# The low part of a weight one step after its cast, and the drain of attention in hand order

## The chip, the cores and the metric

The kernel runs on one core of one Trainium2 chip. The metric is the device time of one execution in microseconds (us). Before the change its median over three runs is 1068.23 us.

## The reference, cut to what matters

Attention with a position bias feeds two feed-forward layers:

```python
scores = q @ k.T * scale + bias(pos)                  # 4 batches, 8 heads, 576 x 576, head size 64
x = softmax(scores) @ v                               # 2304 tokens x 512
h = x @ w_in                                          # 512 -> 2048
g = (a0 + a1*h + a2*h**2 + a3*h**3) / (1 + |b0|*|h| + |b1|*h**2 + 1e-6)
y = g @ w_out                                         # 2048 -> 512
z = maximum(maximum(y @ w1, y @ w2), y @ w3) @ w_out2 # 512 -> 768 -> 512
```

The weights come in double precision, and the matrix products are wanted in full single precision.

## The kernel before

**Precision.** A weight or an activation is split in a high part (a cast to the matmul's format) and a low part (value minus high part). Each product is three matmuls: high times high, high times low, low times high.

**Attention** is a sequence of 80 units, one per batch, pair of heads p and tile of 128 rows t (the last tile, t = 4, holds 64 rows of two heads). `attn_tick(n)` issues the work of tick n in the order of the list `KN['A2']`: scores of unit n (`sc`), a part of an attention-times-value product (`av`), the transposes of unit n-2 (`T`), bias and minimum of unit n (`r0`, `r1`, VectorE), the reciprocal of unit n-1's sums and its spreading on GpSimd (`n`), the exponentials (`e0`, `e1`, ScalarE), and the copies of the transposes out of PSUM (`v0`, `v1`). At the end of a tick come the weights' step, and in ticks 72, 75 and 80 the load and the two splits of the first block's x (`split_x`, L446: a cast on ScalarE, a subtraction on GpSimd for each of four chunks).

**First layer.** `ffn_tick(n)` is one step for chunk f of a block of tokens: the 12 matmuls `ph` of chunk n (`ffn_h`), the 12 matmuls `y` of chunk n-2 (`ffn_y`), then the rational function: `rat_poly(n)`, the cast and low part of g of the chunk before (`rat_split(n-1)`), `rat_inv(n)` and `rat_newton(n)`, and at the end the weights' step. So on ScalarE a step is three activations of `rat_poly`, the cast to gs (L506), Ln, Exp and the weights' instructions; on GpSimd it is the low part of gs (L507) and then the weights' low parts.

**Drain.** After tick 79 no new unit starts, but five more ticks finish the last units. They are ticks 80 to 84, and in each of them `attn_tick(n)` is followed by `ffn_tick(n - 80)`. Both run a weights' step, so there are two weights' steps in such a tick; here they are called a (at the end of the attention's part) and f (at the end of the layer's part).

**Weights.** `weights_tick(new)` advances every weight that is under way by one stage and then starts `new` further loads. Its four stages are: load into one of three raw buffers (SyncE's DMA queue); for a weight in double precision an activation on ScalarE and a shift on VectorE (`rebias`, L387, L388), which need the landed load; joining the two words on VectorE (`join`, L396); then the cast on ScalarE and the low part on GpSimd or VectorE (`parts`, L402). The weights w_in (`wi`, 16 of them) are loaded narrowed already, so their second and third stages are empty; w_out (`wo`, 16) has all four. A raw buffer comes free when the low part is made. The loads of `wi` start in tick 64, one a tick; `wo` follows them. `weights_flush` runs further weights' steps if a chunk's weight isn't there.

**Order.** SyncE's queue is always in program order (L76). Inside `ordered(3)` PE, VectorE, GpSimd and ScalarE are too. Ticks 0 to 79 and the layer's steps from 5 on stand in it; the drain does not, and there a planner that works with modelled times chooses the order on these four engines. Each engine's own queue is then worked off in that order.

**Places.** `big` has two buffers, which hold the transposed attention tiles `at` and, later, the working pair g of the rational function; `slot` has 35 buffers of 4,608 bytes a partition for weights, keys, bias, exponentials and x; `bank` has four PSUM banks for scores' transposes, av, ph and s.

Of the kernel before, what the change touches and what calls it, by code (L numbers as in the profile page):

```python
# [8 lines left out]
F32 = mybir.dt.float32  # L9
# [8 lines left out]
P = 128  # L18
# [8 lines left out]
HID = 32  # L27
TOFF = 572
TW = 1148
KN = {'NSLOT': 35, 'NRAW': 3, 'NRAWX': 2, 'NATT': 4, 'HB': 0, 'NE': 'd', 'FP': 2, 'BL': 4, 'T4': 0, 'LSP': 1, 'KX': 4, 'HT': 'ss', 'EVP': 'da', 'TTP': 'dda', 'NXS': 4, 'EARLY': 0, 'NM0': 0, 'MAN': 3, 'MANF': 3, 'H2': [2, 4, 6, 8, 10, 12, 14, 16], 'SP0': [3, 4], 'BW': 3, 'A2': ['na', 'sc', 'sq1', 'av', 'p1', 'T', 'r0', 'r1', 'n', 'st', 'p2', 'sq', 'e0', 'e1', 'v0', 'v1'], 'LL': 7, 'SL': 3, 'LL0': 9, 'SL0': 4, 'SQ': [1], 'CUT2': 2, 'CUT3': 3, 'WS': 12, 'WE': 70, 'WT': 64, 'XT': 8, 'XA': 3, 'XB': 8, 'F': ['g2a', 'g2d', 'h', 'g1a', 'w', 'g2p', 'g1d', 'g1p', 'y', 'x', 'g3'], 'LOW': 4, 'LOM': 3, 'LOI': 2, 'GHI': 'dve', 'GLO': 'dve', 'BED': 8, 'BE0': 16, 'NU1': 'pool', 'XE': ['act', 'pool'], 'WR': 1, 'YSP': 'act', 'LAG': 2, 'EV1': 'dve', 'XSE': 'act', 'STQ': 'sp', 'PUQ': 'sp', 'NB0': 0, 'HP': 0, 'SB': 2, 'XLA': 3, 'XLB': 6, 'XSA': 11, 'YL': 10, 'YS': 14, 'WLOW': 1}  # L30
REBIAS = 2.0 ** -112
TOSIGN = -2.0 ** 32
QC = 1.0 + 1e-6
# [4 lines left out]
def tile_attention_moe(  # L38
# [25 lines left out]
    def big(name, shape, dt=F32):  # L64
        return sb.tile(shape, dt, tag="big", name=name, bufs=2)
# [7 lines left out]
    def f32(ap):  # L73
        return ap.bitcast(F32)
# [279 lines left out]
    wt_ = {}  # L354
# [17 lines left out]
    def weight_stages(src, name, n, packed=False, lo_eng=pool, narrow=None):  # L372
        box = {}
        wide_ = src.dtype != F32

        def load():
            if wide_:
                box["r"] = raw(f"wr{name}{n}", [P, 512, 2], I32)
                sp.dma_start(box["r"], src[n].bitcast(I32).rearrange("p (c w) -> p c w", w=2))
            else:  # L380
                box["r"] = raw(f"wr{name}{n}", [P, 512], F32)
                sp.dma_start(box["r"], src[n])

        def rebias():
            if wide_:
                low, high = box["r"][:, :, 0], box["r"][:, :, 1]
                act.activation(f32(high), f32(high), AF.Prelu, scale=REBIAS, alpha=TOSIGN)  # L387
                dve.tensor_scalar(low, low, 29, None, ALU.logical_shift_right)  # L388

        def join():  # L390
            if wide_:
                low, high = box["r"][:, :, 0], box["r"][:, :, 1]
                res = low
                if narrow is not None:
                    res = sb.tile([P, 512], I32, tag="xs", name=f"wn{name}{n}", bufs=KN['NXS'])
                dve.scalar_tensor_tensor(res, high, 3, low, ALU.logical_shift_left, ALU.bitwise_or)  # L396
                box["r"] = f32(res)

        def put():
            (act if KN["PUQ"] == "act" else sp).dma_start(narrow[n], box["r"])  # L400

        def parts():  # L402
            weight_place(name, n, packed)
            r, w = box["r"], wt_[name, n]
            if isinstance(w, list):
                for k in range(4):
                    act.copy(w[0][k], r[:, k * P:(k + 1) * P])
                for k in range(4):
                    lo_eng.tensor_tensor(w[1][k], r[:, k * P:(k + 1) * P], f32(w[0][k]), ALU.subtract)
            else:  # L410
                hi, lo = (w[:, 4 * a:4 * a + 4].rearrange("p k c -> p (k c)") for a in range(2))
                act.copy(hi, r)
                lo_eng.tensor_tensor(lo, r, f32(hi), ALU.subtract)

        if narrow is not None:
            return [load, rebias, lambda: (join(), put())]
        return [load, rebias, join, parts]

    pipe, todo = [], []

    def weights_tick(new=1):
        for st in list(pipe):
# [7 lines left out]
                pipe.append(st)  # L430

    def weights_flush(keys):
        while any(k not in wt_ for k in keys):
            weights_tick(1)


# [36 lines left out]
    def rat_poly(blk, f):  # L473
        n = blocks[blk][1]
        ph = ph_t[blk, f][:, :n]
        s = bank(f"s{blk}_{f}")[:, :n]
        bt = big(f"g{blk}_{f}", [P, 2, 512])
        q, u = bt[:, 0, :n], bt[:, 1, :n]
        bun[blk, f] = ph, s, q, u
        act.activation(s, ph, AF.Abs, scale=B0)  # L480
        act.activation(q, ph, AF.Square)  # L481
        dve.scalar_tensor_tensor(q, q, B1, s, ALU.mult, ALU.add)  # L482
        act.activation(u, ph, AF.Identity, scale=A3, bias=A2)  # L483
# [142 lines left out]
    def ordered(m):  # L626
        names = ["SP", "PE", "DVE", "Pool", "Activation"][:(1, 2, 3, 5)[m]]
        return tc.manual_schedule(engines={getattr(mybir.EngineType, e) for e in names})
# [85 lines left out]
    def attn_tick(n):  # L714
        for t, p in bloads_at.get(n, []):
            if (t, p) not in bias:
                bias_load(t, p)
        u0 = units[n] if n < NU else None
        u1 = units[n - 1] if 1 <= n <= NU else None
        u2 = units[n - KN["LAG"]] if KN["LAG"] <= n < NU + KN["LAG"] else None  # L720
        ev = []
        for step in KN["A2"]:
            if step == "sc" and u0:
                if u0[2] == u0[1][0]:
                    at_tiles(u0[0], u0[1], u0[3])
                scores(u0[0], u0[2], u0[3])
            elif step in ("r0", "r1") and u0:
                reduce_min(u0[0], u0[2], u0[3], int(step[1]))
            elif step in ("e0", "e1") and u0 and (step == "e0" or u0[2] < 4):
                expo(u0[0], u0[2], u0[3], int(step[1]))  # L730
            elif step == "st":
                while stq:
                    attn_store(*stq.pop(0))
            elif step == "T" and u2:
                ev = transposes(u2[0], u2[2], u2[3])
            elif step == "na" and u1:
                sum_guard(u1[0], u1[2], u1[3])
            elif step == "n" and u1:
                normalise(u1[0], u1[2], u1[3])
            elif step == "v0" and u2:  # L740
                act.copy(*ev[0])  # L741
            elif step == "v1" and u2:
                for e_ in ev[1:len(ev) - 1]:
                    evac(KN["EVP"][n % len(KN["EVP"])], e_)
                evac(KN["TTP"][n % len(KN["TTP"])], ev[-1])
            elif step in ("p1", "p2"):
                early_pop(n, 0.5 * int(step[1]))
            elif step == "av":
                if avq:
                    av, js = avq.pop(0)  # L750
                    attn_v(*av, js)
                    if 4 in js:
                        stq.append(av)
                if u2 and u2[2] == u2[1][-1]:
                    av = (u2[0], u2[1], u2[3])
                    cuts = {1: (5,), 2: (3, 2), 3: (2, 2, 1)}
                    cut = {1: (5,), 2: cuts[KN["CUT2"]], 3: cuts[KN["CUT3"]]}[len(u2[1])]
                    avq.extend((av, range(sum(cut[:k]), sum(cut[:k + 1]))) for k in range(len(cut)))
            elif step == "sq1":
                for bp in splits_at.get(n, []):  # L760
                    sqq.extend(split_kq(*bp))
                if sqq:
                    sqq.pop(0)()
            elif step == "sq":
                for _ in range(KN["SQ"][n % len(KN["SQ"])]):
                    if sqq:
                        sqq.pop(0)()
        for b, p in loads_at.get(n, []):
            if p % 2 == 0:
                load_v(b, p)  # L770
            load_kq(b, p)
        WT, XT = KN["WT"], KN["XT"]
        if n == WT:
            todo.extend((slim["wi"], "wi", f, True, low_eng(KN["LOI"], f)) for f in range(NF))
        if n >= WT:
            weights_tick(KN["WR"])
        if n == NU - XT:
            load_x("x", x_d, 0, 0)
            load_x("x", x_d, 0, 1)
            todo.extend(wo_todo(f) for f in range(NF))  # L780
        for m, kcs in ((KN["XA"], (0, 1)), (KN["XB"], (2, 3))):
            if n == NU - XT + m:
                for kc in kcs:
                    split_x("x", 0, kc)
# [2 lines left out]
        for n in range(KN["NM0"], NU):  # L787
            attn_tick(n)
    n = NU
    while avq or stq or n < NU + KN['LAG']:  # L790
        attn_tick(n)
        ffn_tick(n - NU)
        n += 1
    n_drain = n - NU

    with ordered(KN["MANF"]):
# [90 lines left out]
```

## Time and profile before

| | |
|---|---|
| time before, median of 3 runs | 1068.23 us (1068.21 to 1068.77) |
| the profiled execution, its own time | 1066.84 us |
| its span from first to last instruction | 1064.9 us |
| mean granted TensorE clock | 0.997 |
| PE busy | 1025.4 us, 96% |
| DVE (VectorE) busy | 662.9 us, 62% |
| ACT (ScalarE) busy | 627.5 us, 59% |
| POOL (GpSimd) busy | 419.9 us, 39% |

1.9 us of the profiled time lie outside the span. The drain lies at about 343 to 389 us of the span: the attention's last products and the first layer's first six chunks.

### The profile page before, as it was taken

To read this page: it belongs to the slowest core of one execution; us is meant where nothing else is said; L and a number is where in the kernel's file an instruction comes from. 1 tells how busy PE (TensorE), PEld (TensorE's weight loads), DVE (VectorE), ACT (ScalarE), POOL (GpSimd) and SP (SyncE) were. 2 spreads that over 40 slices of the span, in tenths; PEclk is the share of its full clock that TensorE was granted. 3 is DMA by queue.
4 is the path that set the end of the run, shared out by engine and by line. 5 is a ranking of instruction groups with operands and counts; after the bars stand their busy time and mean duration, and the time that the engine had idled before them with its cause. 6 is when DMAs were issued, how large, how long until landed. Compare 5 with 4: busy or idle time off the path is not lost. (4 is left out here: it accounts for less than half of the span.)

```text
span 1064.9 us, 16574 instructions
## 1 busy us (share of the span) xinstructions
PE 1025.4 (96%) x5996; PEld 809.9 (76%) x5996; DVE 662.9 (62%) x1307; ACT 627.5 (59%) x1237; POOL 419.9 (39%) x580
## 2 busy tenths in 40 slices
PE   7899999999987799999999999999999999999998
PEld 2267777777765578788899888788888888888887
DVE  8965676767764899877788877799953111111111
ACT  7986676777766778776678667788633211211111
POOL 3007686777684434422234223243623321210211
PEclk9999999999999999999999999999999999999999
DMA  6887655454543432010020200224242200101010
GB/s 244 279 289 205 259 164 187 158 156 170 191 139 113 154 132 91 1 60 1 1 79 2 80 1 1 80 80 138 80 139 99 80 1 20 61 1 60 1 40 20
DMA packets 43394, 107.94 MB, mean 101 GB/s; under 512 B 4784, under 2 KB 11184, under 8 KB 43312
## 3 DMA queue, kind: packets, MB, share of 16 engines
q1 hardware_dynamic: 43312, 106.89, 30.0%
q8 instruction: 47, 0.77, 0.3%
q14 instruction: 35, 0.29, 0.1%
HBM read 77.90 MB, written 28.97 MB: 100 GB/s over the span
## 5 line engine op out<-in xcount | busy, mean ns | idle before, releaser
L459 PE MATMUL p<-ys,wm 128*128 128x512 f32 (+1 forms) x1080 | 227.0, 368 | 0.0
L459 PE MATMUL ph<-xs,wwi 128*128 128x512 f32 (+1 forms) x960 | 214.3, 372 | 5.2 <-ACT at L741 2.4
L459 PEld LDWEIGHTS p<-ys,wm 128*128 128x128 f32 x1080 | 188.9, 188 | 34.3
L459 PE MATMUL y<-gs,wwo 128*128 128x512 f32 (+1 forms) x905 | 204.2, 372 | 1.8 <-POOL gs L507 1.6
L459 PEld LDWEIGHTS ph<-xs,wwi 128*128 128x128 f32 x960 | 168.8, 189 | 39.9 <-ACT at L741 2.6
L507 POOL TENSOR_TENSOR gs<-g,gs 128x512 fp32r<-128x512 f32 (+1 forms) x80 | 96.1, 1202 | 226.7 <-ACT gs L506 165.2
L459 PEld LDWEIGHTS y<-gs,wwo 128*128 128x128 f32 x905 | 158.2, 188 | 35.4 <-POOL gs L507 3.4
L266 ACT ACTIVATE e<-e,st 128x576 f32<-128x576 f32 x144 | 110.8, 772 | 82.9 <-DVE st L260 60.7
L551 POOL TENSOR_TENSOR h2s<-mx,h2s 128x512 fp32r<-128x512 f32 (+1 forms) x30 | 35.5, 1183 | 225.5 <-ACT h2s L550 225.5
L260 DVE CUSTOM_DVE_ANT_0 e<-s,bias 128x576 f32<-128x576 f32 x144 | 103.9, 753 | 19.2 <-PE s L235 7.1
L547 DVE TENSOR_TENSOR mx<-p,mx 128x512 f32<-128x512 f32 (+1 forms) x30 | 19.1, 637 | 141.4 <-PE p L459 137.4
L480 ACT ACTIVATE s<-ph,keep 128x512 f32<-128x512 f32 (+1 forms) x80 | 49.5, 619 | 86.8 <-PE ph L459 86.5
L550 ACT CAST h2s<-mx 128x512 fp32r<-128x512 f32 (+1 forms) x30 | 17.3, 578 | 127.4 <-DVE mx L548 127.4
L235 PE MATMUL s<-k,qs 128*128 128x288 f32 x512 | 85.4, 307 | 2.6 <-DVE st L260 2.2
L301 PEld LDWEIGHTS tp<-ident,e 128*128 128x128 f32 x576 | 61.7, 141 | 32.8 <-issue 17.2
L343 PE MATMUL av<-at,v 128*64 128x320 f32 (+3 forms) x576 | 76.7, 390 | 8.6 <-ACT at L741 6.7
L301 PE MATMUL tp<-ident,e 128*128 128x128 f32 x576 | 80.5, 280 | 0.7 <-DVE xs L349 0.7
L565 PE MATMUL o<-wmo,h2s 128*128 128x512 f32 x324 | 78.6, 390 | 0.0
L482 DVE SCALAR_TENSOR_TENSOR g<-g,keep,s 128x512 f32<-128x512 f32 (+1 forms) x80 | 55.3, 691 | 36.3 <-ACT g L481 34.9
L235 PEld LDWEIGHTS s<-k,qs 128*128 128x128 f32 x512 | 70.3, 189 | 6.0 <-DVE st L260 4.6
L565 PEld LDWEIGHTS o<-wmo,h2s 128*128 128x128 f32 x324 | 60.4, 188 | 12.6 <-POOL h2s L551 0.4
L494 DVE SCALAR_TENSOR_TENSOR g<-g,keep,s 128x512 f32<-128x512 f32 (+1 forms) x80 | 55.5, 694 | 17.9 <-ACT s L488 14.7
(104 smaller groups left out, 1571.8 us busy)
## 6 DMA issues: line engine op xcount, KB each, us to landing
bias_d<-bo SPq DMA_DIRECT2D x36, 288.0 KB, 4.6
kr<-in_k SPq DMA_DIRECT2D x16, 576.0 KB, 4.7
qr<-in_q SPq DMA_DIRECT2D x16, 576.0 KB, 5.1
bias<-bias_d SPq DMA_DIRECT2D x16, 576.0 KB, 5.8
wrm<-in_m SPq DMA_DIRECT2D x18, 512.0 KB, 3.6
wrwin<-in_wi SPq DMA_DIRECT2D x16, 512.0 KB, 4.4
wrwo<-in_wo SPq DMA_DIRECT2D x16, 512.0 KB, 3.6
v<-in_v SPq DMA_DIRECT2D x8, 576.0 KB, 4.9
```

Source lines behind the costliest of these rows:

```text
L235: pe.matmul(pt[:, x, :HS], lhsT=qs[:, u, t * P:(t + 1) * P], rhs=ks[u][:, w, x * HS:(x + 1) * HS], start=w == 0, stop=w == 1,)
L260: dve.tensor_tensor_reduce(out=dst, in0=src, in1=bs, op0=ALU.add, op1=ALU.min, scale=-0.125, scalar=3.0e38, accum_out=st[:, u:u + 1],)
L266: act.activation(et[:, u], et[:, u], AF.Exp, bias=st[:, u:u + 1], scale=-1.0, accum_out=st[:, 2 + u:3 + u])
L301: pe.transpose(tp[:, j * P:(j + 1) * P], flat[:, 640 * u + j * P:640 * u + (j + 1) * P], ident)
L343: pe.matmul(po[r, :n], lhsT=l, rhs=m, start=j == 0, stop=j == 4, skip_group_check=True)
L459: pe.matmul(po, lhsT=wpart(key, a, k), rhs=rhs, start=first and i == 0, stop=last and i == 2)
L480: act.activation(s, ph, AF.Abs, scale=B0)
L482: dve.scalar_tensor_tensor(q, q, B1, s, ALU.mult, ALU.add)
L494: dve.scalar_tensor_tensor(u, u, A0, s, ALU.add, ALU.mult)
L507: pool.tensor_tensor(t[1], u, f32(t[0]), ALU.subtract)
L551: pool.tensor_tensor(t[:, 1], m, f32(t[:, 0]), ALU.subtract)
L565: pe.matmul(po, lhsT=h[:, a, tt * P:(tt + 1) * P], rhs=w[c], start=j == 0 and i == 0, stop=j == NF2 - 1 and i == 2,)
```

## The change

Three things are changed. The third and fourth stage of a weight become `high` (the cast) and `rest` (the low part), in two successive weights' steps; `join` moves into the step of `rebias`, so the number of steps until the low part is made stays the same. `ready` takes the place of `wt_` in `weights_flush`. In ticks 75 and 78 (`W2`) two loads are started in place of one. The drain is put inside `ordered`, so all engines keep program order there. The working pairs of chunks 0, 1 and 2 of the first block (`RS`) get a `slot` in place of a `big` buffer.

```diff
-        def parts():
+        def high():
             weight_place(name, n, packed)
             r, w = box["r"], wt_[name, n]
             if isinstance(w, list):
                 for k in range(4):
                     act.copy(w[0][k], r[:, k * P:(k + 1) * P])
+            else:
+                act.copy(w[:, 0:4].rearrange("p k c -> p (k c)"), r)
+
+        def rest():
+            r, w = box["r"], wt_[name, n]
+            if isinstance(w, list):
                 for k in range(4):
                     lo_eng.tensor_tensor(w[1][k], r[:, k * P:(k + 1) * P], f32(w[0][k]), ALU.subtract)
             else:
                 hi, lo = (w[:, 4 * a:4 * a + 4].rearrange("p k c -> p (k c)") for a in range(2))
-                act.copy(hi, r)
                 lo_eng.tensor_tensor(lo, r, f32(hi), ALU.subtract)
+            ready.add((name, n))
...
-        return [load, rebias, join, parts]
+        return [load, lambda: (rebias(), join()), high, rest]
...
-        while any(k not in wt_ for k in keys):
+        while any(k not in ready for k in keys):
...
-        bt = big(f"g{blk}_{f}", [P, 2, 512])
+        bt = (slot if blk == 0 and f < KN["RS"] else big)(f"g{blk}_{f}", [P, 2, 512], F32)
...
-            weights_tick(KN["WR"])
+            weights_tick(2 if NU - n in KN["W2"] else 1)
...
-    while avq or stq or n < NU + KN['LAG']:
-        attn_tick(n)
-        ffn_tick(n - NU)
-        n += 1
+    with ordered(KN["MANF"]):
+        while avq or stq or n < NU + KN['LAG']:
+            attn_tick(n)
+            ffn_tick(n - NU)
+            n += 1
```

`KN` has `'RS': 3, 'W2': (5, 2)` where it had `'WR': 1`; NU is 80.

## Rows read from the trace of the kernel before

**Rows 1.** Busy time by window: PE, PEld, DVE, ACT, POOL, clock, DMA share, GB/s.

```profile
300.00:360.00 60.00, 49.08 (x334) 34.71 (x334) 35.79 (x91) 41.57 (x97) 35.29 (x64) 1.00 0.45 142
360.00:420.00 60.00, 55.69 (x232) 44.49 (x233) 55.83 (x89) 49.51 (x88) 26.05 (x24) 0.97 0.38 124
420.00:480.00 60.00, 59.72 (x259) 48.04 (x258) 49.45 (x73) 43.85 (x76) 21.93 (x17) 1.00 0.11 36
```

**Rows 2.** Timeline of PE, 343 to 392 us: start, us, line, out<-in [idle before].

```profile
343.78 1.95 PE L343 MATMUL av<-at,v 128*64 128x256 f32 x16 [0.85 <-DVE xs L349]
...
348.03 3.03 PE L459 MATMUL ph<-xs,wwi 128*128 128x512 f32 x12 [0.62 <-DVE xs L349]
...
357.01 2.37 PE L343 MATMUL av<-at,v 128*64 128x320 f32 x16
...
361.71 3.04 PE L459 MATMUL ph<-xs,wwi 128*128 128x512 f32 x12 [1.79 <-DVE g L496]
...
372.30 0.78 PE L459 MATMUL y<-gs,wwi 128*128 128x512 f32 x2 [2.03 <-ACT gs L506]
372.90 4.59 PE L459 MATMUL ph<-xs,wwi 128*128 128x512 f32 x12
...
388.81 2.93 PE L459 MATMUL ph<-xs,wwi 128*128 128x512 f32 x12
391.58 2.95 PE L459 MATMUL y<-gs,wwo 128*128 128x512 f32 x12
```

**Rows 3.** Timeline of SyncE's DMA queue: two of the weights' loads.

```profile
330.41 0.32 SPq L382 DMA_DIRECT2D wrwi<-wi_n  x1
...
391.85 0.33 SPq L379 DMA_DIRECT2D wrwo<-in_wo  x1
```

**Rows 4.** Timeline of POOL: low parts of weights (L409, L413), of x (L451), of gs (L507).

```profile
328.68 1.71 POOL L409 TENSOR_TENSOR wwi<-wrwi,wwi 128x128 fp32r<-128x128 f32 x4 [1.61 <-ACT wwi L407]
...
339.27 1.29 POOL L413 TENSOR_TENSOR wwi<-wrwi,wwi 128x512 fp32r<-128x512 f32 x1 [2.40 <-ACT wwi L412]
...
347.04 2.99 POOL L451 TENSOR_TENSOR xs<-xr,xs 128x512 fp32r<-128x512 f32 x2
...
394.26 1.30 POOL L507 TENSOR_TENSOR gs<-g,gs 128x512 fp32r<-128x512 f32 x1 [4.92 <-ACT gs L506]
```

**Rows 5.** Timeline of DVE: last attention copy of tick 79, a low part, a chunk's last step.

```profile
343.65 0.41 DVE L322 COPY att<-tt 128x256 f32<-128x256 f32 x1
...
391.14 0.68 DVE L413 TENSOR_TENSOR wwo<-wrwo,wwo 128x512 fp32r<-128x512 f32 x1
...
396.76 0.69 DVE L496 SCALAR_TENSOR_TENSOR g<-s,g 128x512 f32<-128x512 f32 x1
```

**Rows 6.** Timeline of ACT: the second split of x, chunk 0, and step 6.

```profile
346.14 1.14 ACT L450 CAST xs<-xr 128x512 fp32r<-128x512 f32 x2
...
351.14 0.66 ACT L480 ACTIVATE s<-ph,keep 128x512 f32<-128x512 f32 x1 [0.33 <-PE ph L459]
...
389.57 0.67 ACT L387 ACTIVATE wrwo<-wrwo 128x512 f32<-128x512 f32 x1
391.78 0.66 ACT L480 ACTIVATE s<-ph,keep 128x512 f32<-128x512 f32 x1 [1.53 <-PE ph L459]
...
393.50 0.62 ACT L506 CAST gs<-g 128x512 fp32r<-128x512 f32 x1
...
394.75 0.58 ACT L488 ACTIVATE s<-s 128x512 f32<-128x512 f32 x1
395.25 0.65 ACT L412 CAST wwo<-wrwo 128x512 fp32r<-128x512 f32 x1
```

**Rows 7.** Loads of wo (L379), 290 to 400 us, from issue to landing.

```profile
DMA to landing us min/median/max: 3.4/3.8/5.7
```

**Rows 8.** Two of the windows of 1 us around PE's wait at 370 us, columns as above.

```profile
371.00:372.00 1.00, 0.00 (x0) 0.00 (x0) 1.00 (x2) 0.97 (x3) 0.14 (x1) 1.00 0.80 217
...
373.00:374.00 1.00, 1.00 (x4) 0.81 (x4) 0.66 (x2) 1.00 (x3) 1.00 (x2) 0.50 1.05 363
```

More of the change, by code (lines that the diff above doesn't have):

```diff
@@ L29 @@
 TW = 1148
-KN = {'NSLOT': 35, 'NRAW': 3, 'NRAWX': 2, 'NATT': 4, 'HB': 0, 'NE': 'd', 'FP': 2, 'BL': 4, 'T4': 0, 'LSP': 1, 'KX': 4, 'HT': 'ss', 'EVP': 'da', 'TTP': 'dda', 'NXS': 4, 'EARLY': 0, 'NM0': 0, 'MAN': 3, 'MANF': 3, 'H2': [2, 4, 6, 8, 10, 12, 14, 16], 'SP0': [3, 4], 'BW': 3, 'A2': ['na', 'sc', 'sq1', 'av', 'p1', 'T', 'r0', 'r1', 'n', 'st', 'p2', 'sq', 'e0', 'e1', 'v0', 'v1'], 'LL': 7, 'SL': 3, 'LL0': 9, 'SL0': 4, 'SQ': [1], 'CUT2': 2, 'CUT3': 3, 'WS': 12, 'WE': 70, 'WT': 64, 'XT': 8, 'XA': 3, 'XB': 8, 'F': ['g2a', 'g2d', 'h', 'g1a', 'w', 'g2p', 'g1d', 'g1p', 'y', 'x', 'g3'], 'LOW': 4, 'LOM': 3, 'LOI': 2, 'GHI': 'dve', 'GLO': 'dve', 'BED': 8, 'BE0': 16, 'NU1': 'pool', 'XE': ['act', 'pool'], 'WR': 1, 'YSP': 'act', 'LAG': 2, 'EV1': 'dve', 'XSE': 'act', 'STQ': 'sp', 'PUQ': 'sp', 'NB0': 0, 'HP': 0, 'SB': 2, 'XLA': 3, 'XLB': 6, 'XSA': 11, 'YL': 10, 'YS': 14, 'WLOW': 1}
+KN = {'NSLOT': 35, 'NRAW': 3, 'NRAWX': 2, 'NATT': 4, 'HB': 0, 'NE': 'd', 'FP': 2, 'BL': 4, 'T4': 0, 'LSP': 1, 'KX': 4, 'HT': 'ss', 'EVP': 'da', 'TTP': 'dda', 'NXS': 4, 'EARLY': 0, 'NM0': 0, 'MAN': 3, 'MANF': 3, 'H2': [2, 4, 6, 8, 10, 12, 14, 16], 'SP0': [3, 4], 'BW': 3, 'A2': ['na', 'sc', 'sq1', 'av', 'p1', 'T', 'r0', 'r1', 'n', 'st', 'p2', 'sq', 'e0', 'e1', 'v0', 'v1'], 'LL': 7, 'SL': 3, 'LL0': 9, 'SL0': 4, 'SQ': [1], 'CUT2': 2, 'CUT3': 3, 'WS': 12, 'WE': 70, 'WT': 64, 'XT': 8, 'XA': 3, 'XB': 8, 'F': ['g2a', 'g2d', 'h', 'g1a', 'w', 'g2p', 'g1d', 'g1p', 'y', 'x', 'g3'], 'LOW': 4, 'LOM': 3, 'LOI': 2, 'GHI': 'dve', 'GLO': 'dve', 'BED': 8, 'BE0': 16, 'NU1': 'pool', 'XE': ['act', 'pool'], 'RS': 3, 'W2': (5, 2), 'YSP': 'act', 'LAG': 2, 'EV1': 'dve', 'XSE': 'act', 'STQ': 'sp', 'PUQ': 'sp', 'NB0': 0, 'HP': 0, 'SB': 2, 'XLA': 3, 'XLB': 6, 'XSA': 11, 'YL': 10, 'YS': 14, 'WLOW': 1}
 REBIAS = 2.0 ** -112
@@ L411, in parts @@
                 hi, lo = (w[:, 4 * a:4 * a + 4].rearrange("p k c -> p (k c)") for a in range(2))
-                act.copy(hi, r)
                 lo_eng.tensor_tensor(lo, r, f32(hi), ALU.subtract)
+            ready.add((name, n))
         if narrow is not None:
             return [load, rebias, lambda: (join(), put())]
-        return [load, rebias, join, parts]
-    pipe, todo = [], []
+        return [load, lambda: (rebias(), join()), high, rest]
+    pipe, todo, ready = [], [], set()
     def weights_tick(new=1):
```

## The prediction

> **What bounds the kernel now.** I read the busy time by window first: PE is the engine to look at, and the question is where it isn't full. From 420 us on it is busy 59.72 of 60 us, while in the two windows before it lacks 10.9 and 4.3 us [rows 1]. So from the end of the drain on a step costs what PE takes, and a microsecond lost or won before that moves the end by the same amount. Next I read PE's timeline through the drain, for the gaps and what ended them [rows 2]. From the first product of tick 80 (343.78) to chunk 6 (388.81), after which the steps follow without gaps, 45.0 us pass. The work in them is about 35: six ph and four y of 2.8 each are 28, the attention products and transposes some 7. So about 10 us can be won there at the most, and nothing but delay in the chain ph, rational function, y decides it. Then I read the queues of ACT, POOL, DVE and SyncE side by side, because the change makes all of them go in program order. There the reader should look at one thing: a weight's load starts in the instant in which the low part that frees its buffer ends. Pool's low part from 328.68 lasts 1.71, and the next load goes out at 330.41; DVE's of 391.14 lasts 0.68, the load goes out at 391.85 [rows 3 to 5]. With three buffers, load i waits for low part i-3, and SyncE stands still until then.
>
> **Low part later, cast and join earlier.** As many instructions as before; no engine does more. The gain is that Pool no longer waits on a cast of its own step: 1.61 and 2.40 us in ticks 75 and 77 [rows 4], with the sums' guards of the attention queued behind it. Bounds: nothing, and the whole 4.0. A walk through the queues brings the attention's end 2.7 us forward, and I take that. Later the same edit is worth nothing, because PE is full there (420 us on, [rows 1]); without that cover it would be the Pool waits again. The join, one step earlier, waits for the activation of its own step, but in a normal step that activation (389.57, 0.67 long) is over before DVE ends its chunk at 391 [rows 5, 6].
>
> **Own places.** With `big` alone, chunk 1 would have to wait in program order for attention products of tick 83. With slots it doesn't. By my count 15 of the 35 slots are free in tick 80, so the places cost nothing; if they were short, ACT would wait in its poly step.
>
> **Two loads in ticks 75 and 78.** The fourth load doesn't fit in three buffers, so from there on the loads are not ahead; each is asked for one step earlier but still waits for the low part i-3. Follow the first w_out weights. wo0 is started in tick 78 and needs the buffer of wi13, whose low part DVE makes in tick 79. The very next instruction in DVE's queue is wo0's shift, which needs the landed load; ACT's activation needs it in the same step. A landing takes 3.4 to 3.8 us, 5.7 at the longest [rows 7]. Both engines stand idle for it. wo1 needs the buffer of wi14, whose low part Pool makes in tick 80, behind the spreading of the reciprocal; that reciprocal stands on DVE behind wo0. So the second landing follows the first, and ACT waits for it ahead of the second split of x, which chunk 0's ph needs.
>
> The sum, from the end of tick 79 on DVE: 343.65 + 0.41 = 344.06 [rows 5], less 2.7, plus a low part of 0.68 gives 342.0. Landing of wo0, 3.8: 345.8. Activation 0.67 [rows 6] and a join of the size of the low part, 0.68: 347.1. Reciprocal and its copies on Pool, estimated at 0.6, and a low part of 1.29 [rows 4]: 349.0. Landing of wo1: 352.8. Activation: 353.5. Then the split of x. Before, its cast began at 346.14 and the rational function of chunk 0 at 351.14, 5.0 later [rows 6], of which Pool was late by about 0.4: so 4.6. Chunk 0's function starts at 358.0, against 351.14: **6.9 us later**.
>
> **The drain in hand order.** Now there are two weights' steps between one chunk and the next, with this cycle, each link of which stands in the program order: cast of gs (n-1), its low part on Pool, behind it the low part of the weight in step f, which frees the buffer for the load, the landing, ACT's activation for that load in step a of the next tick, and only then chunk n+1's function on ACT. From the rows of step 6: function's start 391.78 to the end of the gs cast 394.12 [rows 6] is 2.34; Pool's low part ends at 395.56 [rows 4], 1.44 later; a weight's low part 1.29; landing 3.4 to 3.8; activation 0.67. That makes 9.1 to 9.5, where PE needs 5.5 (388.81 to 391.58, twice, [rows 2]). The cycle binds chunks 1 to 4, three times: 3 x 9.3 = 28. From chunk 0 to chunk 1 a low part on DVE stands in it after the chunk's last step: 391.78 to 397.45 is 5.7 [rows 5, 6], plus 0.68, 3.8 and 0.67: 10.8; some of these 5.7 are the steady step's own waits, so I take 10.4. From chunk 4 to 5 there is no wait: to the end of Exp 3.55, cast and activation some 1.25 [rows 6], 4.8.
>
> Chunk 5's function starts at 358.0 + 10.4 + 28 + 4.8 = 401.2, its cast of gs(4) ends 2.34 later, and y of chunk 4 can start at 403.6. Before it started at 391.58 [rows 2]. **12.0 us later**, and from there PE is full. Against the profiled execution's own time (1066.84: span 1064.9 and 1.9 around it) that is 1078.8; the median lies 1.4 above that execution, so 1080.
>
> Bounds: with 3.4 for each of the six landings 1.8 goes off (0.4 three times, 0.2 in each cycle), and with all 4.0 of Pool's waits won 1.3 more: +8.9. With two of the landings at 5.7 and nothing won early: 3.8 and 2.7 more, +18.5.
>
> **The clock.** PE's clock fell to 0.50, the 1.2 GHz level, at 373 us, after a stretch in which PE did nothing (371 to 372), and a ph took 4.59 in place of about 2.9 [rows 2, 8]. A fall between chunks 0 and 1 would be covered (PE has 4.6 us of work in 10.4). In the three cycles it has 6.8 of 9.3 and would need 13 or so at half clock: up to 4 each.
> The Trainium skill, TensorE: Matmul & The Clock Gate, section HAM oscillation, says that an engine that waits on loads between bursts is throttled again and starts every burst slow. By that rule all three cycles would take 13 and the sum would be about +24 in place of +12. The trace agrees only in part, since PE also waited 1.79 ahead of 361.71 [rows 2] and its next ph took no longer.
>
> **Rivals.** 1. The two extra loads do what they look like and wo0 and wo1 are in place when asked for, but the cycle binds. Then chunk 0 starts at about 349.5 (ACT is free at 343, the split and its 4.6 follow): 349.5 + 43.2 + 2.34 = 395.1, +3.5 to +4: 1072. For it: the step is asked for earlier. Against it: loads and low parts in one instant [rows 3 to 5].
> 2. The two waits are there, the cycle isn't (landings are over before ACT asks). Chunk 0's ph ends at 358, the PE work until chunk 6 is 9 x 2.8 and 5.0, and 0.8 of waiting for the first gs: 389.0, +0.2: 1068, no change.
> 3. The other side: neither binds, the weights arrive in time, and hand order merely takes the planner's detours away. ph of chunk 0 ends at 349.4, 31.0 more give 380.4 against 388.81: -8.4, 1060. It decides if every landing is covered by a spare step, as in the steady steps (load at 391.85, asked for one step of 5.5 later). For it: the gaps of today come from orders that nobody chose (1.79 and 2.03, [rows 2]). Against it: two weights' steps in one tick and three buffers.
> 4. Half clock in the cycles, as above: 1084 to 1095.
>
> **How the numbers follow.** My forecast, +8.9 to +18.5, 1077 to 1087: 0.58. Rival 1: 0.14. Rival 2: 0.07. Rival 3: 0.15. Rival 4: 0.06. Hence slower 0.78, same 0.07 (within 0.2%, 2 us, about what a measurement of this kernel tells from none), faster 0.15. The time is that of the forecast, 1080. A range from 1066 to 1089 holds the forecast, rivals 1 and 2 and the lower part of 4, about 0.8; the forecast's own range is 1077 to 1087.
>
> **What would show it.** DVE and ACT idle for 3.4 us or more before wo0's shift in tick 79, ACT again before wo1's activation; the second split of x near 353, and chunk 0's function near 358. Chunks 1 to 4 some 9 us apart, each after an L387 that waited for a load. Wrong if the functions follow each other every 5.5 to 6 us, if no L387 waits, or if a load goes out ahead of low part i-3. Pool's waits on casts in ticks 75 and 77 should be gone in any case.

## The result and the profile after

The changed kernel takes 1080.73 us (median of 4 runs, 1077.76 to 1082.44) against 1068.5 for the kernel before on the same chip: ratio 1.0111, 95% interval 1.0088 to 1.0134. That is **slower by 12.2 us**, where +12.0 was forecast. The profiled execution, the fastest of the four, took 1077.76 with a span of 1075.7, 10.8 more than the span before, at a mean clock of 0.993.

The busy time by window answers to [rows 1] (same columns):

```profile
300.00:360.00 60.00, 46.17 (x302) 31.86 (x302) 35.09 (x88) 41.59 (x96) 36.44 (x66) 0.94 0.45 141
360.00:420.00 60.00, 54.81 (x221) 40.80 (x222) 49.78 (x80) 43.46 (x79) 21.95 (x20) 0.94 0.39 128
420.00:480.00 60.00, 59.71 (x259) 48.10 (x258) 49.56 (x74) 43.35 (x75) 21.91 (x17) 1.00 0.10 35
```

From 420 us on PE is as full as before; the loss lies in the first two windows, and in both the clock is lower than before too. PE's timeline through the drain, to be laid beside [rows 2], shows what stopped it:

```profile
341.76 1.51 PE L343 MATMUL av<-at,v 128*64 128x256 f32 x12
...
350.99 0.80 PE L465 MATMUL ph<-xs,wwi 128*128 128x512 f32 x1 [4.79 <-ACT xs L456]
352.33 2.50 PE L465 MATMUL ph<-xs,wwi 128*128 128x512 f32 x5 [0.55 <-POOL xs L457]
...
358.34 0.33 PE L307 MATMUL tt<-ident,e 128*128 128x128 f32 x1 [0.99 <-DVE g L496]
...
360.15 4.59 PE L465 MATMUL ph<-xs,wwi 128*128 128x512 f32 x12 [1.37 <-ACT at L747]
...
386.90 4.37 PE L465 MATMUL y<-gs,wwo 128*128 128x512 f32 x11 [0.90 <-POOL gs L513]
...
396.02 2.82 PE L465 MATMUL y<-gs,wwo 128*128 128x512 f32 x11 [0.91 <-POOL gs L513]
398.68 2.93 PE L465 MATMUL ph<-xs,wwi 128*128 128x512 f32 x12
401.45 2.95 PE L465 MATMUL y<-gs,wwo 128*128 128x512 f32 x12
```

The first product of tick 80 is 2.0 us earlier (341.76 for 343.78), and y of chunk 4 is 9.9 later (401.45 for 391.58). Between the two stand a wait of 4.79 for the second split of x, and later waits for g that comes too slowly. Why the split is late stands in ACT's timeline. Read the L387 rows: that activation needs a landed load.

```profile
346.80 0.69 ACT L387 ACTIVATE wrwo<-wrwo 128x512 f32<-128x512 f32 x1 [1.36 <-DMA wrwo<-in_wo]
348.25 0.65 ACT L409 CAST wwo<-wrwo 128x512 fp32r<-128x512 f32 x1 [0.76 <-DVE wrwo L396]
349.75 0.68 ACT L387 ACTIVATE wrwo<-wrwo 128x512 f32<-128x512 f32 x1 [0.84 <-DMA wrwo<-in_wo]
350.32 1.13 ACT L456 CAST xs<-xr 128x512 fp32r<-128x512 f32 x2
354.93 0.66 ACT L486 ACTIVATE s<-ph,keep 128x512 f32<-128x512 f32 x1 [3.48 <-PE ph L465]
...
363.73 0.68 ACT L387 ACTIVATE wrwo<-wrwo 128x512 f32<-128x512 f32 x1 [0.83 <-DMA wrwo<-in_wo]
364.77 0.66 ACT L486 ACTIVATE s<-ph,keep 128x512 f32<-128x512 f32 x1 [0.37 <-PE ph L465]
...
366.50 0.62 ACT L512 CAST gs<-g 128x512 fp32r<-128x512 f32 x1
...
368.79 0.69 ACT L387 ACTIVATE wrwo<-wrwo 128x512 f32<-128x512 f32 x1
371.61 0.69 ACT L409 CAST wwo<-wrwo 128x512 fp32r<-128x512 f32 x1 [2.13 <-DVE wrwo L396]
373.11 0.68 ACT L387 ACTIVATE wrwo<-wrwo 128x512 f32<-128x512 f32 x1 [0.82 <-DMA wrwo<-in_wo]
373.68 0.66 ACT L486 ACTIVATE s<-ph,keep 128x512 f32<-128x512 f32 x1
```

The last four rows are one cycle of the drain: the join's result is awaited (2.13), then a landing (0.82), and the next chunk's function follows. GpSimd frees the buffer, and SyncE sends the load that was awaited:

```profile
367.20 1.30 POOL L513 TENSOR_TENSOR gs<-g,gs 128x512 fp32r<-128x512 f32 x1 [6.96 <-ACT gs L512]
368.45 1.33 POOL L418 TENSOR_TENSOR wwo<-wrwo,wwo 128x512 fp32r<-128x512 f32 x1
```

```profile
369.81 0.33 SPq L379 DMA_DIRECT2D wrwo<-in_wo  x1
```

The low part ends at 369.78, the load goes out at 369.81, and it is used at 373.11, 3.3 later.

The chunks of all kernels that matter below, by the start of the rational function on ACT (us of the span):

| chunk | 0 | 1 | 2 | 3 | 4 | 5 | 6 |
|---|---|---|---|---|---|---|---|
| before | 351.1 | 359.7 | 366.8 | 372.2 | 378.6 | 384.6 | 391.8 |
| after | 354.9 | 364.8 | 373.7 | 383.1 | 392.2 | 395.1 | 402.4 |
| e1 one load | 350.1 | 360.5 | 369.6 | 378.9 | 388.2 | 391.0 | 399.0 |
| e3 all in slots | 352.7 | 363.4 | 371.4 | 380.0 | 388.0 | 390.2 | 398.3 |
| e9 one step | 351.7 | 362.5 | 367.3 | 374.3 | 380.8 | 386.3 | 392.5 |
| e12 layer later | 354.7 | 359.3 | 365.0 | 370.4 | 375.3 | 383.1 | 388.9 |
| e14 and wi in slots | 352.2 | 356.8 | 362.5 | 367.9 | 372.8 | 380.6 | 386.4 |

### The profile page after: what moved, and what is told of

Its sections match the earlier page's. It is cut to its first block, busy times and chain, and to the rows that moved or that the text cites. A ratio compares the mean times of both kernels' runs of the same rounds, so it can differ in the third digit from the quotient of the medians.

```text
span 1075.7 us, 16594 instructions
## 1 busy us (share of the span) xinstructions
PE 1031.8 (96%) x5996; PEld 811.0 (75%) x5996; DVE 662.8 (62%) x1307; ACT 626.2 (58%) x1237; POOL 417.0 (39%) x580
## 5 line engine op out<-in xcount | busy, mean ns | idle before, releaser
L465 PE MATMUL y<-gs,wwo 128*128 128x512 f32 (+1 forms) x905 | 206.4, 375 | 5.2 <-POOL gs L513 2.9
L486 ACT ACTIVATE s<-ph,keep 128x512 f32<-128x512 f32 (+1 forms) x80 | 49.3, 616 | 79.7 <-PE ph L465 79.4
```

The costliest lines, as they stand in the source:

```text
L465: pe.matmul(po, lhsT=wpart(key, a, k), rhs=rhs, start=first and i == 0, stop=last and i == 2)
```

## The experiments

The theory is that of the forecast: two landings ahead of chunk 0, then a cycle through the raw buffers in chunks 1 to 4. The rival is that the buffers only show last, and that the order itself (two weights' steps in a tick, in program order on all engines) costs the time. Each run is compared with the kernel before on the same chip.

| run | median us | ratio | 95% interval |
|---|---|---|---|
| e1 one load | 1073.80 | 1.0051 | 1.0033 to 1.0069 |
| e2 planner | 1073.74 | 1.0053 | 1.0036 to 1.0070 |
| e7 order only | 1076.24 | 1.0084 | 1.0069 to 1.0099 |
| e8 split only | 1070.49 | 1.0022 | 1.0010 to 1.0034 |
| e3 all in slots | 1074.67 | 1.0063 | 1.0041 to 1.0084 |
| e4 late in slots | 1076.65 | 1.0081 | 1.0061 to 1.0100 |
| e9 one step | 1072.21 | 1.0045 | 1.0027 to 1.0063 |
| e10 later cast | 1086.27 | 1.0173 | 1.0143 to 1.0203 |
| e11 later cast, ten | 1071.82 | 1.0032 | 1.0016 to 1.0048 |
| e12 layer later, slots | 1066.39 | 0.9984 | 0.9970 to 0.9998 |
| e13 layer later | 1066.90 | 0.9990 | 0.9975 to 1.0005 |
| e14 and wi in slots | 1064.22 | 0.9964 | 0.9951 to 0.9978 |

**Which part of the change costs it.** e1 starts one load in every tick; e2 leaves the drain to the planner.

```diff
-'W2': (5, 2)
+'W2': ()
```

> The changed kernel with one load in ticks 75 and 78 again (W2 empty). Theory (waits on landed loads: two ahead of chunk 0, then a cycle of landing and low part between chunks 1 and 4): the two waits ahead of chunk 0 go, its function starts near 349.5 us in place of 354.9, chunk 1 follows after 6 to 7 us since the low part on DVE no longer stands between them, and chunks 1 to 4 stay about 9.1 us apart. In all 1070 to 1075 us against 1080.7. Rival A (the two extra loads help, the hand order alone costs): 1080 or more. Rival B (half clock of PE is the cost, not the waits): chunk 0 starts earlier, but the time moves by less than 2 us.

```diff
-    with ordered(KN["MANF"]):
-        while avq or stq or n < NU + KN['LAG']:
-            attn_tick(n)
-            ffn_tick(n - NU)
-            n += 1
+    while avq or stq or n < NU + KN['LAG']:
+        attn_tick(n)
+        ffn_tick(n - NU)
+        n += 1
```

> The changed kernel with the drain left to the planner, as before; split stages, extra loads and own places stay. Theory: nearly all of the loss is the hand order meeting full raw buffers, so the time comes back to the kernel before, 1066 to 1070 us. Rival (the split stages or the extra loads cost by themselves): 1075 us or more.

e7 is the kernel before with the drain in `ordered` and slots for the g of chunks 0 to 2, so the order alone. e8 is the change with the planner's drain, one load a tick and no slots for g, so the split of cast and low part alone.

> The kernel before with the drain in hand order and own places for chunks 0 to 2 alone; stages and loads as before. Theory (two weights' steps in a tick are too much for the hand order, whatever the stages): chunks 1 to 4 are 8 to 10 us apart and the time is 1073 to 1079 us. Rival (the join moved beside its activation, or the low part moved, is at fault): below 1071 us.

> The kernel before with the split stages alone (low part one step after the cast, join one step earlier); one load a tick, the planner's drain, all working pairs in the big buffers. Theory: Pool's waits on casts in ticks 75 and 77 go, the attention ends 1 to 2.5 us earlier, and the planner's drain stays about as it was: 1064 to 1068 us. Rival (the split itself disturbs the drain): 1070 us or more.

The order alone costs 0.84%, the split alone 0.22%, the split with the extra loads (and the slots for g) 0.53% under the planner. In hand order the split earns (0.51% for 0.84%) and the extra loads cost (1.11% for 0.51%). The parts don't add up as three sums would: what one of them costs depends on which chain it finds binding. In e1 chunk 0 starts at 350.06, 4.9 earlier than with the extra loads, without a wait at an L387 ahead of it: so the two landings ahead of chunk 0 come from the extra loads. Chunk 1 follows after 10.4, where 6 to 7 was expected. The three cycles (9.1, 9.3, 9.3) are as long as after the change: they don't come from the extra loads. In e7, with the old stages, the cycles are as long (9.7, 9.6, 9.8 from chunk 1 to 4), and ACT's waits for a landing 1.9 to 2.2 us each. That a planner's drain with the new stages is slower than before was not expected, in e2 or in e8. In e8 the loads are awaited again, and PE's timeline shows one of the delays:

```profile
356.53 4.40 PE L465 MATMUL ph<-xs,wwi 128*128 128x512 f32 x12 [3.43 <-ACT at L747]
```

The copy of the last transposes was put behind more work on ACT than before. Why the planner orders it so stays open.

A rival runs through the smaller of these differences: the granted clock. Among the runs of the kernel before beside these experiments (13, 15, 24 and 17 runs), a mean clock lower by 0.001 goes with 0.4 to 0.9 us more, group by group. The median clock was 0.9925 in e8 for 0.995 before, 0.993 in e2 for 0.996, 0.997 in e14 for 0.996. So 1.0 to 2.2 of e8's 2.5 us go with the clock. Its profiled execution shows the clock at 0.61 from 304 to 308 us and 0.72 from 334 to 340, where that of before has 1.00. What the split itself costs under the planner is therefore not settled.

**What binds the cycle.** e3 gives the raw words of wo0 to wo9 a slot each, so their loads wait for no low part; e4 does it from wo2 on.

```diff
-                box["r"] = raw(f"wr{name}{n}", [P, 512, 2], I32)
+                box["r"] = (slot if name == "wo" and 0 <= n < 10 else raw)(f"wr{name}{n}", [P, 512, 2], I32)
```

> The changed kernel with the raw tiles of wo0 to wo9 in the free slots, so that a load no longer waits for a low part. Theory: both the waits ahead of chunk 0 and the cycle go; chunk 0 starts near 349.5, chunks follow each other every 5.5 to 6.5 us, no activation L387 waits for a landing in ticks 79 to 84; 1061 to 1066 us, below the kernel before. Rival A (hand order itself, the load on ACT and DVE of two weights' steps in a tick): chunks stay 8 to 9 us apart, 1075 us or more.

> The changed kernel with the raw tiles of wo2 to wo9 alone in free slots; wo0 and wo1 wait for a raw buffer as in the changed kernel. Theory: the two waits ahead of chunk 0 stay (chunk 0 near 355), the cycle goes (5.5 to 6.5 us a chunk); 1067 to 1071 us. Rival A (hand order itself): 1078 us or more. If the two pieces add up, its loss and that of the run with one load in ticks 75 and 78 together make the whole loss.

In e3 the landings are gone from the cycles, but the loss falls from 12.2 to 6.7 us only (the span of the profiled execution is 4.1 shorter). One L387 ahead of chunk 0 still waits 2.04 for a landing, against the expectation, and chunk 0 starts at 352.7. The cycle goes from 8.9, 9.4 and 9.1 to 8.0, 8.6 and 8.0. ACT's timeline shows what lay 1 us below:

```profile
370.22 0.70 ACT L409 CAST wwo<-wrwo 128x512 fp32r<-128x512 f32 x1 [2.15 <-DVE wrwo L396]
370.82 0.70 ACT L387 ACTIVATE wrwo<-wrwo 128x512 f32<-128x512 f32 x1
371.42 0.65 ACT L486 ACTIVATE s<-ph,keep 128x512 f32<-128x512 f32 x1
```

e4 keeps the two waits ahead of chunk 0 (355.6) and has the same cycles, 8.0, 8.5 and 8.0, where 5.5 to 6.5 was expected. Its loss (8.6) and that of e1 (5.8) make 14.4 where the whole is 12.2, so the two pieces don't add up.

The same wait for L396 stands in the rows of after (2.13). In step f the shift and the join stand on DVE behind the chunk's tail; the cast of the very next step a needs that join; and behind the cast on ACT stand L387 and the next function. From the rows of after: function 364.77, the tail on DVE ends 370.44 (5.7 later), shift and join 1.1, cast 0.6, L387 0.6: 8.0. So two steps in one tick bind the chunks at 8.0 without any DMA. That calls for two tests. e9 (on top of e3) lets the attention's part of a drain tick do no weights' step. e10 and e11 (on top of e3) keep two steps, but with an empty stage between join and cast for all `wo`, or for the first ten.

```diff
-        if n >= WT:
+        if WT <= n < NU:
```

> The changed kernel with raw tiles of wo0 to wo9 in free slots, and in ticks 80 to 84 one weights' step in place of two (that of the layer's part). New theory: with the landings covered, the chunks are 8 us apart because the cast of a weight on ACT waits for the join on DVE, which stands behind the whole tail of the chunk before; with one step a tick the join has a whole chunk's time. Then chunks 1 to 4 follow each other every 5.5 to 6.5 us, no cast waits for a join, 1064 to 1069 us. Rival (ACT and DVE simply have too much to do in hand order, or PE's half clock): 7.5 us or more a chunk, 1072 us or more.

```diff
+        if name == "wo":
+            return [load, lambda: (rebias(), join()), lambda: None, high, rest]
         return [load, lambda: (rebias(), join()), high, rest]
```

> The changed kernel with raw tiles of wo0 to wo9 in free slots and an empty stage between join and cast of a wo; all work and both weights' steps in a tick stay. New theory (a cast on ACT waits for a join behind the tail of the chunk before): the cast now finds its join done, and the chunks follow each other every 5.8 to 6.8 us in place of 8.0; 1065 to 1070 us. Rival (the load of two weights' steps on ACT and DVE): 7.5 us or more a chunk, 1073 us or more.

e11 has the same edit with `if name == "wo" and n < 10:`.

> The run with the later cast, but the empty stage only for wo0 to wo9, whose raw tiles lie in slots; the weights after them, which share three raw buffers, keep four stages. Theory (the five stages in three buffers made the waits of 4 to 6 us after 405 us): these waits go, the drain's gain stays, 1069 to 1072 us. Rival (the later cast doesn't help): 1074 us or more.

All three shorten the cycles: 4.9, 7.0, 6.5 in e9, 5.7, 8.4, 7.1 in e10 and e11. So the join does bind. The middle cycle of e10 and e11 hardly moves (8.4 for 8.6); in e11 PE is busy without a gap from 369 to 379 us there, so it costs PE nothing. In e10 the price is paid later. From wo10 on, five stages have to live in three raw buffers, and PE falls to 72.33 busy of 80 us from 405 on, where it had 79.7:

```profile
409.82 0.67 ACT L387 ACTIVATE wrwo<-wrwo 128x512 f32<-128x512 f32 x1 [4.39 <-DMA wrwo<-in_wo]
...
420.25 0.67 ACT L387 ACTIVATE wrwo<-wrwo 128x512 f32<-128x512 f32 x1 [5.76 <-DMA wrwo<-in_wo]
```

e11 limits the empty stage to weights with slots and keeps the gain, 14 us better than e10. e9 stays above what was expected of it: the weights arrive later than y wants them, with PE 77.34 busy of 80 from 405 on and 2.4 us of y waiting for low parts of wo.

**Chunk 0 to chunk 1.** In after, e1, e3, e4, e9, e10 and e11 it takes 8.0 to 10.7 us. The rows of PE after show another cause beside the weights: the transposes of tick 81 wait for a PSUM bank that DVE's L496 frees (0.99), and ph of chunk 1 for ACT's copy of them (1.37), which stands behind Ln and Exp of chunk 0 and a weight's cast and L387. e12 (on top of e3) starts the layer one tick later and makes one weights' step a tick from there on. e13 does it without slots for the raw words.

```diff
-        if n >= WT:
+        if WT <= n <= NU:
...
-            ffn_tick(n - NU)
+            if n > NU:
+                ffn_tick(n - NU - 1)
...
-    n_drain = n - NU
+    n_drain = n - NU - 1
```

> The changed kernel with raw tiles of wo0 to wo9 in slots, the layer starting one tick later (its step 0 beside tick 81 and behind tick 81's transposes and copies) and one weights' step a tick from tick 81 on. Theory (chunk 1's ph waits for a PSUM bank that a copy frees which stands on ACT behind chunk 0's function; the cycles need two weights' steps a tick): chunks follow each other every 5.5 to 6.3 us from chunk 0 on, chunk 6 starts before 390 us, 1060 to 1066 us, faster than the kernel before. Rival (hand order leaves chunk 1 late anyway): chunk 1 9 us or more after chunk 0, 1069 us or more.

> The same without the slots for raw tiles. Theory: the two waits on landed loads ahead of chunk 0 stay (chunk 0 near 354 to 357), the cycle doesn't come back because one load a tick has a whole step to land: 1063 to 1069 us. Rival (three raw buffers bind in any hand order): chunks 8 us or more apart, 1072 us or more.

From chunk 0 to 1 it is now 4.6 us in both, and chunks 1 to 4 follow in 4.9 to 5.7. e13 needs no extra places and is level with before, so three raw buffers don't bind in every hand order. e12 is faster by 0.16%, with an interval that ends at 0.02%; its median clock was 0.996 for 0.995, so it may be level too. What held e12 then was its start. ACT waits for a landing ahead of the second split of x. wo0 has a slot, but in SyncE's queue its load stands behind those of `wi`, which still share the three raw buffers:

```profile
347.72 0.70 ACT L387 ACTIVATE wrwo<-wrwo 128x512 f32<-128x512 f32 x1 [2.27 <-DMA wrwo<-in_wo]
```

e14 (on top of e12) gives the loads of wi11 to wi15 slots too, so the loads of wo0 and wo1 no longer stand behind a wait for the low parts of `wi`.

```diff
-                box["r"] = raw(f"wr{name}{n}", [P, 512], F32)
+                box["r"] = (slot if name == "wi" and n >= 11 else raw)(f"wr{name}{n}", [P, 512], F32)
```

> The shifted version with slots, and the raw loads of wi11 to wi15 in slots too, so that no cast of a weight near chunk 0 waits for a landing. Theory (the 2.27 us wait for a landing ahead of chunk 0 in the shifted version is what holds chunk 0's function at 354.7): no such wait, chunk 0's function near 350.5 to 352.5, 1062 to 1065 us, faster than before. Rival (chunk 0 is held by the split of x and the copies of attention anyway): chunk 0's function at 354 or later, 1065.5 us or more.

```profile
344.76 0.69 ACT L387 ACTIVATE wrwo<-wrwo 128x512 f32<-128x512 f32 x1
...
347.60 0.66 ACT L387 ACTIVATE wrwo<-wrwo 128x512 f32<-128x512 f32 x1
348.16 1.13 ACT L456 CAST xs<-xr 128x512 fp32r<-128x512 f32 x2
352.19 0.66 ACT L486 ACTIVATE s<-ph,keep 128x512 f32<-128x512 f32 x1 [2.26 <-PE ph L465]
```

No L387 waits, chunk 0's function starts 2.5 earlier than in e12, and the time is 1064.22: **0.36% faster than before**, where the change was 1.11% slower. (Some 0.4 to 0.9 of its 3.2 us go with the higher clock.) Of what is won in the drain not all arrives. y of chunk 4 starts 7.3 us earlier than before (384.30), the span ends 3.6 earlier. Part of it shows in PE's timeline at the split of the second block's x, for which PE now waits:

```profile
440.50 0.96 PE L465 MATMUL ph<-xs,wwi 128*128 128x512 f32 x3 [0.53 <-POOL xs L457]
441.74 0.74 PE L465 MATMUL ph<-xs,wwi 128*128 128x512 f32 x2 [0.28 <-POOL xs L457]
```

Laid beside the kernel before, matmul by matmul, the lead of 7.3 at y of chunk 4 is 5.9 by 436 us, lost in the y of these steps, two of which wait for the low part of g. At the split it falls to 4.8. It stays there up to the first product of the second layer (p, 754.34 for 759.17) and falls to 3.65 in that layer's first steps, where p waits for the split of its input and, at 771.91, 0.28 for a copy on ACT. From there to the end nothing is lost.

## Why the forecast held, step by step

The cycle through the raw buffers was right, link by link. That the total came out at 12.2 for 12.0 is in part luck: a term ahead of chunk 0 was too large, one at the end too small, one came near by another path, and the medians hold something that no term had.

- **Low part later.** Right: Pool's waits on casts of their own step are gone (one of 0.74 on a cast of the step before is left, at 338.69). Tick 80's first product starts 2.0 earlier, where 2.7 was taken; counted from 290 us, where the changed kernel stood 0.7 behind, it is 2.8.
- **Own places.** No run has the hand order without them, so this term was not tested.
- **Loads follow low part i-3.** Right in that each load waits for a low part, but not always for that one. wi15's low part stands in step f, on DVE behind the whole of chunk 0. wo2's load didn't wait for it; it took wo0's buffer and went out at 354.79, as Pool's low part of wo0 ended (353.47 + 1.30) and 6.3 ahead of the end of wi15's (361.06). That is one of the forecast's own signs of being wrong. From wo5 on, in the cycles, the rule holds. The landings took 3.2 to 4.4 us, 3.4 in the middle (290 to 400 us), against 3.4 to 5.7 and 3.8 [rows 7].
- **Two landings in series ahead of chunk 0.** This was the term furthest off. Both waits are there (1.36 and 0.84 on ACT), but the split's cast starts at 350.32 and not near 353, and chunk 0's function at 354.9 and not 358.0: 3.8 late where 6.9 was forecast. wo0's own part was as forecast: its load went out at 342.91 (342.0) and landed in 3.8. The step that failed is "that reciprocal stands on DVE behind wo0". DVE's timeline has it ahead:

```profile
343.01 0.16 DVE L275 RECIPROCAL st<-st 128x1 f32<-128x1 f32 x1
344.33 0.69 DVE L322 COPY at<-tp 128x512 f32<-128x512 f32 x1 [1.16 <-PE tp L301]
346.78 0.43 DVE L388 TENSOR_SCALAR wrwo<-wrwo 128x512 int32<-128x512 int32 x1 [1.75 <-DMA x_d<-xs]
```

Ticks 79 and 80 lie in two `ordered` blocks, and at their border this row of tick 80 was placed ahead of the last of tick 79. So Pool could make the low part of wi14 at once, and wo1's load left at 345.27 (forecast: 349.0), while wo0's was still on its way:

```profile
343.95 1.29 POOL L418 TENSOR_TENSOR wwi<-wrwi,wwi 128x512 fp32r<-128x512 f32 x1 [0.18 <-ACT wwi L409]
```

The landings overlapped. (The 1.75 ahead of L388 is put down to another transfer; on ACT the same load ends a wait in the same moment.)

- **Split to chunk 0's function, 4.6.** Measured 350.32 to 354.93, 4.6, though with PE at half clock. The clock's share is some 0.5, an estimate: ph ends 1.3 after the last low part of x (353.51 to 354.83), and 0.8 after it in e14, at the upper level.
- **Chunk 0 to 1, 10.4.** Measured 9.84, near the forecast by luck, since the path was another. The load that L387 awaits at 363.73 went out at 360.26, when Pool ended the low part of wo1, which had waited for that weight's cast behind chunk 0's Exp. DVE's low part, the forecast's link, ended at 361.06 and freed a buffer that chunk 1's function didn't wait for:

```profile
359.77 0.47 POOL L415 TENSOR_TENSOR wwo<-wrwo,wwi 128x128 fp32r<-128x128 f32 x1
```

```profile
360.38 0.68 DVE L418 TENSOR_TENSOR wwi<-wrwi,wwi 128x512 fp32r<-128x512 f32 x1
```

The landing (L387 ends at 364.4) and ph (ends at 364.7) come out almost together. The forecast had only the first; e3 and e12 show that the second, transposes and their copy behind chunk 0's work, holds it as well.
- **The cycle, 9.3 three times.** Measured 8.9, 9.4 and 9.1, each with a landing awaited at L387. The links of the first, from 364.77: to the end of the gs cast 2.35 (forecast 2.34), its low part 1.38 (1.44), the weight's 1.28 (1.29), load to use 3.33 (3.4 to 3.8), activation 0.57 (0.67). What the forecast didn't see is the chain of the join 1 us below. It changes nothing in the sum, but it is why taking the cycle through the raw buffers away in e3 brought so little.
- **From chunk 4 to y(4).** Forecast 4.8 and 2.34, 7.1 together; measured 392.2 to 401.45, 9.2. Chunk 5's function came earlier than thought (395.06), but y of chunk 3 and ph of chunk 6 stand ahead of y(4) on PE, and y(3) had itself waited for gs until 396.02. The sum stepped from ACT to PE without asking what PE still had to do.

So -3.1 at chunk 0, -1.1 in the chunks and +2.1 at the end made y(4) 401.45 in place of 403.6. The forecast for the profiled execution was 1078.8 and it took 1077.76. Another 0.9 of its 10.8 arises in the second layer (its first product is 9.8 later than before, the last of the output 10.7) and was in no term. Between the profiled executions the loss is 10.9 us, between the medians 12.2: the other three runs of the change are 3.0 to 4.7 slower than its profiled one, with mean clocks of 0.987 to 0.989 for 0.993. That was in no term of the sum either.

**The rivals.** Rival 1 (loads in place, the cycle binds, 1072) is almost what e1 is: 1073.8. Rivals 2 and 3 needed chunks that follow one another in about 5.5; that takes e12's order, not this one. The price of rival 3, 1060, was not reached by e14 either. Rival 4's upper end, 1095, is more than its own sum gives (1080 and three times 4). On that rival the profiled execution shows the clock at 0.50, the 1.2 GHz level, from 350 to 356 us, where it fell during PE's wait of 4.79, and again from about 360 to 363 and from 387 to 391, in the ph at 360.15 and the y at 386.90. Their twelve and eleven matmuls take 4.59 and 4.37 where 3.0 and 2.8 are usual. In the other cycles it stays at the upper level or comes back, and from 391 to 396 us it is 1.00. The Trainium skill, TensorE: Matmul & The Clock Gate, section HAM oscillation, tells of a kernel in which every burst after a wait for loads starts slow. These three bursts agree; the one after the wait of 0.91 ahead of 396.02 doesn't, its eleven matmuls took 2.82, the upper level. By that rule the sum was +24. What the two falls in the chunks cost the path here is 0.4 at most (ACT's wait for the slow ph ahead of 364.77), since chunk 4's function at 392.22 waited for a landing and not for the slow y. The four runs of after spread over 4.7 us, the slower ones with the lower clock; where in those runs it fell, no trace shows.

## What to carry to other kernels

A load that is issued earlier gains nothing when its buffer isn't free: follow the load to the instruction that frees its buffer, and ask what is queued behind the consumer, on every engine that goes in program order. Two pipeline steps in one tick turn "ready in the next step" into "ready at once", and the chain that shows in the waits may hide another 1 us shorter; before removing the one, work out the length of the next. Spreading the stages over one step a tick and starting the layer a tick later did more here than the places for the loads (e13 is level with before, e3 is 0.63% slower), and only with the order mended did the places pay (e14).

## What the runs showed of the hardware

DVE's shift of the raw words (L388, 128x512 int32) takes 0.42 to 0.43 us when GpSimd is idle. Where GpSimd was at work as it started, it took 0.57 to 1.44 and ended 0.28 to 0.30 after GpSimd's instruction, in 9 of 9 such cases between 340 and 480 us of before, after, e3 and e14. The two rows of e14 that show it, of DVE and of POOL:

```profile
432.31 1.16 DVE L388 TENSOR_SCALAR wrwo<-wrwo 128x512 int32<-128x512 int32 x1
```

```profile
431.89 1.29 POOL L457 TENSOR_TENSOR xs<-xr,xs 128x512 fp32r<-128x512 f32 x1 [0.99 <-ACT xs L456]
```

GpSimd ends at 433.18, the shift at 433.47. The Trainium skill, SBUF — State Buffer, section Who interferes with whom, says that the two engines share a pair of ports under an exclusive lock; these rows agree. In the change it made one shift of the three cycles 0.6 longer (1.00 at 379.27) and cost nothing, since ACT waited for a landing afterwards (0.79 ahead of 382.54). In e3, where the join binds, the cycle with the long shift (1.02 at 377.00) is the one of 8.6 in place of 8.0.
